# Another order of the first steps, and other due times, in a fused linear-attention and feed-forward kernel

## The chip, the cores and the metric

The kernel runs on one core of one Trainium2 chip. The metric is the time of one execution on the device in microseconds. The times of the kernel before are 523.04, 523.28 and 522.9 us, median 523.04. Profiles are of one execution; their times count from the first instruction.

## The reference

A gated linear attention over 4 batches, 8 heads, 768 steps and heads of 48, then a feed-forward layer with a squared ReLU over the 3072 tokens of 384 numbers that the attention leaves.

```python
for t in range(S):                                   # attention: q, k, v, alpha are (4, 8, 768, 48)
    state = alpha[:, :, t, :, None] * state + einsum('bhd,bhe->bhde', k[:, :, t], v[:, :, t])
    y[:, :, t] = einsum('bhd,bhde->bhe', q[:, :, t], state)
x = y.transpose(0, 2, 1, 3).reshape(3072, 384)
h = maximum(x @ w_in, 0.0)                           # w_in (384, 2048)
out = (h * h) @ w_out                                # w_out (2048, 384), both given in float64
```

## The kernel before

**Blocks.** The attention is cut into 24 blocks of 128 steps: block n is chunk n // 4 of batch n % 4. In a block the decays are handled by logarithms. `ln` takes them (ACT, line 242), `cs` sums them over the steps with a triangular matrix on TensorE, `eb` and `ei` make the factors b and 1/b from the sums on ACT, `mq` and `mk` multiply q and k by them on VectorE (line 284). `qT` and `kT` turn q and k on TensorE, `qc` and `kc` copy them out of PSUM. `sc` makes the scores, `kv` the sums of the state, `am` copies the scores through a mask, `us` adds the state, and `st` (next_state, line 414) makes the state of the next chunk. For `st` the last row of b is needed as a column: `bl` writes that row to DRAM (line 297, "row"), `br` reads it back spread over partitions (line 303, "last"), in two DMAs of single numbers. `ya` and `yb` make the output of two blocks, `ev` copies it out of PSUM into x, the operand of the feed-forward layer (line 515), by ACT and, for the first two pairs, also by VectorE. b lies in two buffers that take turns (line 275), so `eb` of block n waits until `mq` and the row of block n - 2 are done with one.

**Groups.** Four blocks, one of each batch, make a group: 512 tokens. The feed-forward layer takes group after group, six in all, 16 columns j of w_in of 128 each, then the product with w_out. While TensorE works on group g, the attention of group g + 1 is made between its matmuls.

**Weights.** The float64 weights come in 16 pieces of 768 KB and are turned into float32 by `first` and `second` on VectorE (lines 153 to 182) with `middle` on ACT between them (lines 166, 169). Group 0 uses them as float32 matmuls of two passes each (line 805, line 701 with w_out), but for a last part. From group 1 on, the numbers are split into a large and a small part and their difference (`prepare`, line 580: cast_w and scale_w on ACT, rest_w and diff_w on VectorE), and a product is three float32r passes (line 622, line 701). The split weights are kept in DRAM and streamed back by SP (`stream`, `pump`). x and h are split too (`split_x`, `split_h`, `diff_h`, on ACT and VectorE).

**What sets the order.** The kernel writes out its own schedule; every engine works its instructions off in the order in which the program gives them, SP its DMA issues too.

- The first four blocks are a list of words (line 851). A word is a step and its block: `mk0` is mk of block 0, `load2a` loads alpha of block 2, `weights0` loads the next piece of weights, `first0`, `middle0`, `second0` turn piece 0, `ha1` and `hb1` are the first and second half of the 512 tokens for column 1, `zeros2` is a filler: a matmul by zeros, three times, six passes in the trace (line 338); `warm0` is one more (line 221).
- From then on `weave` (line 923) goes through a list of units of TensorE's work, each with a cost, and puts steps with a due time between them. Units in groups 1 to 5 are some 1.3 us. `attention` (line 889) gives the due times of a pair of blocks from a start t: the turn of q and k (`turn`, line 474) at 6.5, their eight copies (line 490) at 7, `ga` (scores and sums of the first block, and the output of the pair before) and `gb` (the same of the second) at the values in AT, or at 9.5 and 10.5 times a scale in group 0.
- AT (line 19) holds the numbers. `g0`, `g1`, `g`: starts of the pairs in group 0, group 1 and later ones. `sc0`: scale in group 0. `w_first`, `w_in_at`, `w_in_by`, `wstep`, `o0`, `o2`: when the pieces of weights are split. `g0x`, `g1x`, `xs`: when x of the next group is split. `h0`, `h1by`, `s0`, `ahead`: how early h is split. `str1`: when a stream begins. `tp`: for each of four columns, in groups 2 to 5, which engine squares: with A, ACT scales in PSUM, takes the ReLU and squares; with M, VectorE squares; with D, ACT copies out and VectorE adds, takes the ReLU and squares. `evs0`: spacing of the evictions in group 0. `late` is used only if group 0 is float32 throughout, which it isn't.

Of the kernel before, what the change touches and what calls it, by code (L numbers as in the profile page):

```python
# [15 lines left out]


GB = 4
AT = {'evs': 0.4, 'lead': 4, 'post': 3, 'w_first': (46.0, 49.5, 53.0), 'wstep': 1.6, 'w_in_at': 2, 'w_in_by': 3.4, 'room1': 22, 'room': 25, 's0': 4, 'ahead': 6, 'late': 2, 'xs': 0.2, 'g0': (-0.5, 19.5, 28.0), 'sc0': (2.35, 2.35, 2.35), 'g1': (2.5, 19.5, 35.0), 'g': (2.2, 15.0), 'g1x': 50, 'gx': 46, 'g0x': 55.5, 'k0': 2, 'h0': 18, 'k1': 4, 'h1': 4, 'h1by': 2, 'evs0': 0.8, 'tp': 'ADMD', 'tp1': 'ADAD', 'split': 8, 'o0': (40, 47), 'o1': (), 'o2': (23, 26, 29, 35, 42, 36), 'str1': 24, 'ga': 10, 'gb': 12.5}


RUN = {0: 128, 32: 32, 64: 64, 96: 32}
# [3 lines left out]
def kernel(  # L26
# [220 lines left out]

    SPLIT = AT["split"]

# [290 lines left out]
    here, todo, room = {}, [], [22]  # L540
# [27 lines left out]
    def diff_w(w, p):  # L568
# [5 lines left out]
        for x in "ld":  # L574
            t = made.pop((x, w, p))
            if w == "i" or p >= NW - AT["k0"] or (x == "l" and p >= NW - AT["k1"]):
                here[x, w, p] = t
        pump()

    def prepare(at, w, p):  # L580
        step = AT["wstep"]
        fs = (cast_w, rest_w, scale_w, diff_w)
        return [(at + i * step, f, (w, p)) for i, f in enumerate(fs)]
# [78 lines left out]
    def splits_of_x(at, g):  # L662
        return [(at + i * AT["xs"], f, (g, i % KM)) for i, f in enumerate((split_x,) * KM + (diff_x,) * KM)]

    def layer_in(g):
        units = []
        for n in range(NJ + 2):
            if n < NJ:
                units.append((1.05, in_x, (n,)))
            if 0 <= n - 2 < NJ:  # L670
                units.append((0.53, in_y, (n - 2,)))
            if 0 <= n - AT["post"] < NJ:
                units.append((0, in_post, (n - AT["post"],)))
            if AT["lead"] <= n < AT["lead"] + AHEAD and (g > 1 or AT["k1"] == NW):
# [145 lines left out]
    def ffn_out(g, t, i):  # L820
# [28 lines left out]
    steps["hb"] = lambda j: ffn_in(0, j, slice(HT, 2 * HT))  # L849
    steps["first"], steps["middle"], steps["second"] = convert_first, convert_middle, convert_second  # L850
    first = """
        ln0 cs0 ei0 mk0 warm0 eb0 bl0 mq0 kT0 load0v kc0 ln1 qT0 load2a load2k cs1
        eb1 qc0 mq1 sc0 bl1 kv0 qT1 load1v ei1 mk1 load2q load3a kT1 ln2 qc1 load3k
        cs2 br0 am0 kc1 eb2 sc1 weights0 br1 us0 kv1 zeros2 bl2 load2v am1 ei2 us1
        load3q ya0 ln3 cs3 yb0 eb3 weights1 mk2 ei3 load3v mq2 qT2 st0 ev0 kT2
        zeros2 zeros2 zeros2 kc2 first0 mk3 middle0 kT3 mq3 br2 load4v qc2 kc3 bl3
        weights2 qT3 sc2 load4q qc3 kv2 second0 am2 br3 first1 sc3 weights3 us2
        load4a kv3 am3 us3 load4k middle1 ha1 second1 ya2 yb2 ev2 weights4 first2
        ha0 hb1 middle2 hb0 st2 st3 st1
    """  # L860
    for word in first.split():
        f = max((x for x in steps if word.startswith(x)), key=len)
# [167 lines left out]
```

## Time and profile before

| what | us |
|---|---|
| median of three runs | 523.04 |
| span of the profiled execution | 520.6 |
| difference, outside the span | 2.4 |
| TensorE busy | 510.8 |
| VectorE busy | 366.0 |
| ACT busy | 313.0 |
| end of the last matmul | 517.1 |

The page's first part gives the busy time of each engine, the second its share in 40 slices of 13 us. The list of who waited for whom has four parts: the instruction that waited, what released it, and then the sum, the number of times and the longest. A line of a timeline has start, duration, engine, line of the kernel, operation and tiles; behind "x" the number of instructions that were put together, and in brackets the idle time before them and what ended it. The chain of waits has start, duration and name. In a stage table each engine has its busy time in the stage; the last numbers are the granted clock, the share of the 16 DMA engines and GB/s.

### The profile page before, as it was taken

What the parts mean: (1) busy time and instruction counts of PE and PEld (TensorE: products, weight loads), DVE (VectorE), ACT (ScalarE), POOL (GpSimd) and SP (SyncE); (2) the same over time, 40 slices, a digit from 0 to 9 for tenths busy, and PEclk for the clock granted to TensorE, in tenths of its full rate; (3) what the DMA queues carried; (4) which work ended last, traced back from release to release, by engine and by line L of the source; (5) the groups of instructions that cost most, each with busy time, mean ns of one, the idle gap of its engine ahead of it and who ended that gap; (6) DMA issues with size and microseconds to landing.
All of it is one profiled execution on the core that took longest, in us unless ns stands there. A gap on an engine that the chain in (4) does not pass through costs nothing.

```text
span 520.6 us, 12925 instructions
## 1 busy us (share of the span) xinstructions
PE 510.8 (98%) x5276; PEld 418.2 (80%) x5276; DVE 366.0 (70%) x631; ACT 313.0 (60%) x650; POOL 5.4 (1%) x29
## 2 busy tenths in 40 slices
PE   7989999999999999999999999999999999999997
PEld 4754455668887668988899988899988899988997
DVE  4798989979978787867597476587465476363861
ACT  4668785677888594575963275963275763164620
POOL 4000000000000000000000000000000000000000
PEclk9999999999999999999999999999999999999999
DMA  9999687244686787898884788964673534898201
GB/s 161 209 278 213 196 240 218 60 114 176 224 200 196 195 246 198 264 317 206 195 248 148 251 246 198 230 187 150 231 255 126 179 126 151 268 340 293 70 0 62
DMA packets 140995, 102.36 MB, mean 197 GB/s; under 512 B 111476, under 2 KB 114568, under 8 KB 140936
## 3 DMA queue, kind: packets, MB, share of 16 engines
q1 hardware_dynamic: 140936, 101.53, 68.3%
q8 instruction: 42, 0.69, 0.6%
q14 instruction: 17, 0.14, 0.1%
HBM read 84.18 MB, written 17.33 MB: 195 GB/s over the span
## 4 chain that ended last, share of the span: by engine, by line
PE 93%; DVE 2%; SPq 2%; DMA 1%; issue 1%; POOL 1%; ACT 0%; POOLq 0%; DVEq 0%
PE o L701 41%; PE h L622 32%; PE h L805 7%; PE y L352 4%; PE T L482 2%; PE sckv L372 2%; PE sckv L395 2%; PE cs L265 1%; DMA qk_lent<-in_q_dram 1%; SPq L303 1%; SPq L109 1%; PE cs L268 1%; PE cs L269 1%; DVE x L515 0%; DVE w_in L182 0%
## 5 line engine op out<-in xcount | busy, mean ns | idle before, releaser
L622 PE MATMUL h<-xa,wb 128*128 128x512 f32 x240 | 68.2, 392 | 0.0
L622 PE MATMUL h<-xl,wl 128*128 128x512 f32 x240 | 67.9, 391 | 0.0
L622 PE MATMUL h<-xd,wd 128*128 128x512 f32 x240 | 67.3, 396 | 0.0
L515 ACT COPY x<-y 32x256 f32<-32x256 f32 (+2 forms) x132 | 47.2, 366 | 25.4 <-PE y L352 20.1
L547 DVE TENSOR_TENSOR hid<-h,hid 128x512 f32<-128x512 f32 x40 | 27.6, 689 | 45.5 <-PE h L622 45.4
L701 PE MATMUL o<-wb,ha 128*128 128x384 f32 x160 | 54.6, 342 | 0.0
L701 PE MATMUL o<-w_out,hid 128*128 128x384 f32 x160 | 54.0, 491 | 0.0
L701 PE MATMUL o<-wd,hd 128*128 128x384 f32 x304 | 53.8, 334 | 0.0
L701 PE MATMUL o<-wl,hl 128*128 128x384 f32 x160 | 53.5, 335 | 0.0
L639 ACT ACTIVATE h<-h 128x512 f32<-128x512 f32 x40 | 23.3, 582 | 49.7 <-PE h L622 49.7
L622 PEld LDWEIGHTS h<-xl,wl 128*128 128x128 f32 x240 | 45.1, 188 | 10.0 <-DVE xl L547 0.4
L701 PEld LDWEIGHTS o<-wd,hd 128*128 128x128 f32 x304 | 52.7, 188 | 0.3 <-DVE osb L737 0.3
L622 PEld LDWEIGHTS h<-xa,wb 128*128 128x128 f32 x240 | 44.6, 188 | 9.3 <-ACT xa L596 0.2
L622 PEld LDWEIGHTS h<-xd,wd 128*128 128x128 f32 x240 | 44.2, 188 | 9.2
L701 PE MATMUL o<-wb,hx 128*128 128x384 f32 x144 | 48.7, 338 | 0.0
L701 PE MATMUL o<-wl,hx 128*128 128x384 f32 x144 | 48.1, 334 | 0.0
L701 PEld LDWEIGHTS o<-w_out,hid 128*128 128x128 f32 x160 | 29.8, 190 | 19.3
L637 ACT ACTIVATE hid<-h 128x512 f32<-128x512 f32 x40 | 24.0, 600 | 34.6 <-PE h L622 34.5
L805 PE MATMUL h<-x,w_in 128*128 128x512 f32 (+1 forms) x108 | 43.6, 552 | 1.2 <-ACT x L515 1.2
L596 ACT ACTIVATE ha<-hid 128x512 fp32r<-128x512 f32 x40 | 25.6, 639 | 25.5 <-DVE hx L547 16.1
L805 PEld LDWEIGHTS h<-x,w_in 128*128 128x128 f32 x108 | 19.9, 190 | 21.1 <-issue 17.2
L547 DVE TENSOR_TENSOR hl<-hid,ha 128x512 fp32r<-128x512 f32 x40 | 27.5, 688 | 10.1 <-ACT ha L596 10.1
(114 smaller groups left out, 879.7 us busy)
## 6 DMA issues: line engine op xcount, KB each, us to landing
wd<-do SPq DMA_DIRECT2D x36, 384.0 KB, 3.7
wl<-lo SPq DMA_DIRECT2D x34, 384.0 KB, 4.0
wl<-li SPq DMA_DIRECT2D x32, 384.0 KB, 3.5
wd<-di SPq DMA_DIRECT2D x32, 384.0 KB, 3.9
raw<-in_moe_w_in_dram SPq DMA_DIRECT2D x8, 768.0 KB, 5.6
raw<-in_moe_w_out_dram SPq DMA_DIRECT2D x8, 768.0 KB, 5.6
v_in<-in_v_dram SPq DMA_DIRECT2D x24, 192.0 KB, 4.7
out_dram<-osb SPq DMA_DIRECT2D x24, 192.0 KB, 1.9
```

Of the source, the lines that this page charges most:

```text
L352: ins = nc.tensor.matmul(out=ys[e][64 * half : 64 * half + D + G * e, m % 2, p // 2, t], lhsT=lhsT, rhs=rhs, start=(half, e) not in seen, ...
L372: nc.tensor.matmul(out=ps[e][HALF[h], 0, p, :], lhsT=ks[rows, p, HALF[h]], rhs=qs[rows, p, HALF[h]], start=True, stop=True, skip_group_che ...
L395: nc.tensor.matmul(out=ps[h][64 * e : 64 * (e + 1), 1, p, G:64], lhsT=tile_of("k", n)[HALF[h], 2 * p + e, :], rhs=tiles["v"][n % NV][HALF[ ...
L482: nc.tensor.transpose(out=ps[h][:, i, p, :], in_=rows[HALF[h], 128 * p : 128 * (p + 1)], identity=ident[HALF[h], HALF[h]],)
L515: copy(out=x[kk][to : to + m, t : t + 2], in_=blk[n]["y"][e][r : r + m, :, p // 2],)
L547: nc.vector.tensor_tensor(out=o, in0=x, in1=z, op=op)
L596: nc.scalar.activation(out=a, in_=x, func=AF.Copy, scale=NEAR)
L622: nc.tensor.matmul(out=acc["h", j], lhsT=here[w, "i", p][:, kk, jj * 128 : (jj + 1) * 128], rhs=x_parts[x][:, kk], start=start and kk == 0 ...
L637: nc.scalar.activation(out=hid[j], in_=x, func=AF.Copy, scale=E)
L639: nc.scalar.activation(out=x, in_=x, func=AF.Copy, scale=1.0 + E)
L701: nc.tensor.matmul(out=acc[t][:, 0:DM], lhsT=lhs[:, t * C : (t + 1) * C], rhs=rhs, start=start, stop=stop, skip_group_check=True,)
L805: nc.tensor.matmul(out=ps, lhsT=w[:, kk, c0 : c0 + 128], rhs=xT[g][kk][:, cols], start=(kk == 0), stop=(kk == KM - 1),)
```

## The change

The list of the first steps is put in another order, with five fillers of zeros for four and without `warm0`, and numbers in AT are changed. No step of the computation is added or taken away, but with `tp` DDMD for ADMD the columns 0, 4, 8 and 12 of groups 2 to 5 go from A to D.

In the new list row 1 (`bl1`) is issued behind the first weights, `cs3` and `cs2` stand ahead of `ya0`, `ev2` stands ahead of `second1`, `ha1` and `ha0` behind `yb2`, and the loads of block 3 ahead of the second piece of weights.

```diff
-AT: w_first (46.0, 49.5, 53.0), wstep 1.6, w_in_at 2, w_in_by 3.4, s0 4, ahead 6, late 2, xs 0.2,
-    g0 (-0.5, 19.5, 28.0), sc0 (2.35, 2.35, 2.35), g1 (2.5, 19.5, 35.0), g1x 50, g0x 55.5, h0 18,
-    h1by 2, evs0 0.8, tp 'ADMD', o0 (40, 47), o2 (23, 26, 29, 35, 42, 36), str1 24, ga 10, gb 12.5
+AT: w_first (46.67, 46.11, 53.52), wstep 1.47, w_in_at 2.47, w_in_by 3.41, s0 2, ahead 20, late 1, xs 0.0,
+    g0 (-0.15, 20.48, 28.0), sc0 (2.35, 2.26, 2.35), g1 (5.52, 23.0, 35.06), g1x 51.48, g0x 56.25, h0 15,
+    h1by 1, evs0 1.07, tp 'DDMD', o0 (40.37, 47.68), o2 (29.94, 22.86, 12.71, 31.3, 38.86, 26.77),
+    str1 15.34, ga 8.47, gb 12.26
     first = """
-        ln0 cs0 ei0 mk0 warm0 eb0 bl0 mq0 kT0 load0v kc0 ln1 qT0 load2a load2k cs1
-        eb1 qc0 mq1 sc0 bl1 kv0 qT1 load1v ei1 mk1 load2q load3a kT1 ln2 qc1 load3k
-        cs2 br0 am0 kc1 eb2 sc1 weights0 br1 us0 kv1 zeros2 bl2 load2v am1 ei2 us1
-        load3q ya0 ln3 cs3 yb0 eb3 weights1 mk2 ei3 load3v mq2 qT2 st0 ev0 kT2
-        zeros2 zeros2 zeros2 kc2 first0 mk3 middle0 kT3 mq3 br2 load4v qc2 kc3 bl3
-        weights2 qT3 sc2 load4q qc3 kv2 second0 am2 br3 first1 sc3 weights3 us2
-        load4a kv3 am3 us3 load4k middle1 ha1 second1 ya2 yb2 ev2 weights4 first2
-        ha0 hb1 middle2 hb0 st2 st3 st1
+        ln0 load0v zeros2 cs0 ei0 eb0 zeros2 mk0 kT0 mq0 bl0 load3a load2a load1v ln1
+        br0 cs1 eb1 ei1 qT0 load2k load2q weights0 zeros2 mq1 qc0 kc0 bl1 qT1 sc0 kv0
+        qc1 mk1 kT1 kc1 sc1 am0 load3k us0 st0 load3q ln3 kv1 am1 ln2 us1 cs3 cs2 eb3
+        load2v ya0 ei2 yb0 mk2 eb2 ei3 mq2 zeros2 load3v weights1 kT2 ev0 first0 load4a
+        qT2 mk3 middle0 kT3 mq3 qT3 kc2 bl3 zeros2 qc2 second0 br1 sc2 qc3 kc3 bl2 sc3
+        br2 am2 kv3 am3 kv2 us2 us3 ya2 yb2 first1 st1 middle1 ev2 second1 ha1 br3 ha0
+        st2 weights2 weights3 load4v hb1 load4q first2 st3 load4k hb0 middle2 weights4
     """
```

(The numbers of AT that stay are left out.)

More of the change, by code (lines that the diff above doesn't have):

```diff
@@ L18 @@
 GB = 4
-AT = {'evs': 0.4, 'lead': 4, 'post': 3, 'w_first': (46.0, 49.5, 53.0), 'wstep': 1.6, 'w_in_at': 2, 'w_in_by': 3.4, 'room1': 22, 'room': 25, 's0': 4, 'ahead': 6, 'late': 2, 'xs': 0.2, 'g0': (-0.5, 19.5, 28.0), 'sc0': (2.35, 2.35, 2.35), 'g1': (2.5, 19.5, 35.0), 'g': (2.2, 15.0), 'g1x': 50, 'gx': 46, 'g0x': 55.5, 'k0': 2, 'h0': 18, 'k1': 4, 'h1': 4, 'h1by': 2, 'evs0': 0.8, 'tp': 'ADMD', 'tp1': 'ADAD', 'split': 8, 'o0': (40, 47), 'o1': (), 'o2': (23, 26, 29, 35, 42, 36), 'str1': 24, 'ga': 10, 'gb': 12.5}
+AT = {'evs': 0.4, 'lead': 4, 'post': 3, 'w_first': (46.67, 46.11, 53.52), 'wstep': 1.47, 'w_in_at': 2.47, 'w_in_by': 3.41, 'room1': 22, 'room': 25, 's0': 2, 'ahead': 20, 'late': 1, 'xs': 0.0, 'g0': (-0.15, 20.48, 28.0), 'sc0': (2.35, 2.26, 2.35), 'g1': (5.52, 23.0, 35.06), 'g': (2.2, 15.0), 'g1x': 51.48, 'gx': 46, 'g0x': 56.25, 'k0': 2, 'h0': 15, 'k1': 4, 'h1': 4, 'h1by': 1, 'evs0': 1.07, 'tp': 'DDMD', 'tp1': 'ADAD', 'split': 8, 'o0': (40.37, 47.68), 'o1': (), 'o2': (29.94, 22.86, 12.71, 31.3, 38.86, 26.77), 'str1': 15.34, 'ga': 8.47, 'gb': 12.26}
 RUN = {0: 128, 32: 32, 64: 64, 96: 32}
```

## The prediction

> **What bounds the kernel now.** I read the page first (busy shares, slices), then who waited for whom on TensorE, the chain of waits up to 45 us, and the timelines of the engines over the same stretch.
>
> ```profile
> span 520.6 us, 12925 instructions
> ...
> PE 510.8 (98%) x5276; PEld 418.2 (80%) x5276; DVE 366.0 (70%) x631; ACT 313.0 (60%) x650; POOL 5.4 (1%) x29
> ...
> PE   7989999999999999999999999999999999999997
> ```
>
> TensorE is busy 98% of the span, and 90% or more of every slice between the third and the last. Its instructions stay the same but for fillers, so time can only come out of its waits, or out of new ones. Its waits:
>
> ```profile
> PE h L805 <- ACT x L515: 1.2, 3, 0.7
> PE warm L221 <- POOL s L67: 1.1, 1, 1.1
> PE y L352 <- issue: 1.0, 1, 1.0
> ```
>
> The span less the busy time is 9.8 us. Of it 3.5 us are the stores after the last matmul (517.1), 1.0 us is the wait named "issue" at 203 us, which no semaphore explains, 5.0 us lie before 35.3 us, and 0.3 are scattered. In that first stretch fillers hide more. The chain of waits there, start and duration of each piece:
>
> ```profile
> 18.25 5.06 DMA qk_lent<-in_q_dram
> ...
> 23.81 0.95 DVE power L175
> 24.76 0.88 DVE w_in L179
> 25.66 0.96 DVE w_in L182
> ...
> 31.18 0.96 DVE w_in L182
> ...
> 32.17 0.42 DVE x L515
> ...
> 35.29 9.72 PE h L805 x26
> ```
>
> A load is followed by VectorE alone. VectorE's timeline has it working without a break of 0.3 us from the eviction of blocks 0 and 1 (18.87, six copies) to 41.5:
>
> ```profile
> 17.86 0.36 DVE L421 TENSOR_TENSOR s<-s,last 128x192 f32<-128x192 f32 x1 [1.41 <-DMA last<-row]
> 18.87 2.65 DVE L515 COPY x<-y 32x256 f32<-32x256 f32 x6 [0.65 <-PE y L352]
> ```
>
> From 35.29 TensorE runs through. 26 passes stand there: 8 halves of 0.216 us are left of columns 0 and 1, so **column 2 (j=2) starts at 35.29 + 1.7 = 37.0 us**. This time, less what waits come after it, is what the change can move.
>
> **Part 1, the order of the first four blocks.** I call X the start of VectorE's eviction ev0 (18.87 now) and ask when X comes and how long column 2 is behind it.
>
> *X.* In the new order three things lie ahead of it. (a) Two fillers stand around cs0, six passes each. While the first passes run, one takes 2.93/6 = 0.49 us, later 1.56/6 = 0.26:
>
> ```profile
> 1.09 2.93 PE L221 MATMUL warm<-s 128*128 128x256 f32 x6 [1.09 <-POOL s L67]
> 4.33 1.62 PE L265 MATMUL cs<-a_in,causal 128*128 128x384 f32 x2 [0.31 <-POOL causal_r L204]
> ...
> 14.11 1.56 PE L338 MATMUL zeros<-s 128*128 128x256 f32 x6
> ```
>
> So the first filler ends at about 3.8 + 5 x 0.43 + 0.26 = 6.2, cs0 then takes 0.81 (the later rows' time) and ei0 starts at 7.05 rather than 5.99; b of block 0 is there at 7.9. (b) In SP's queue row 0 waits for that b, and behind it now stand a3, a2, v1, last 0 (two), k2, q2, the first weights, and only then row 1; before, row 1 was issued at 9.45, ahead of all of these but a2 and k2. (c) ACT's eb2 writes the buffer of b that row 1 is read from, so it waits until row 1 has landed; mq2 needs eb2, and ev0 stands behind mq2 on VectorE. A small load moves 197 KB; between 2 and 7 us the DMA engines moved 199 GB/s, between 11 and 15 us 187: 1.03 us each. The weights move 786 KB at 344 to 377 GB/s (18:20, 24:25): 2.2 us. v0 landed at 10.3. Then 5 loads (5.2), the weights (2.2), last (0.3, by its 384 small pieces against a load's 1024), and 0.4 of gap while SP waits for b: row 1 lands at 18.4. eb2 0.45, mq2 0.5: **X = 19.35**, 0.5 later than now. ln3 and ln2, which now wait for a3 until 16.70, no longer set it.
>
> [...]
>
> *Behind X.* VectorE's queue, with the rows' spacing: ev0 2.65, first half of weights 0 1.0, mk3 and mq3 1.0, second half 2.75, both masks (am2, am3) 1.35, us2 and us3 0.75 with the wait for kv2: 9.5. The products end 1.73 behind us3, as now (29.42 to 31.15): X + 11.2. ev2 follows at once (2.65), because the second half of weights 1 now stands behind it (2.8): X + 16.7. TensorE meanwhile does columns 0 and 1 in one run (24 halves, 5.2 us, X + 16.4), where it now has 1.2 us of waits for x. So column 2 starts at X + 16.7 = 36.05, against 37.0 now (X + 18.1): **-0.95 us**. Its next need, weights 2, comes at X + 22.0 on VectorE against X + 21.8 on TensorE, within 0.2, and weights 3 at X + 26.1 against 27.0: nothing is given back. The two extra filler matmuls (6 passes more of zeros, 2 fewer of warm) lie ahead of loads and are in X.
>
> *Bounds.* If SP stalls as it does now at last 0 (2.31 us for one issue, DMA then at 84 GB/s in 15:18), row 1 lands 1.5 later: +0.55. If row 1 isn't what ends last, X is 18.15 (us1 behind last 0, y behind it): -2.1.
>
> **Part 2, the splits of x ahead of group 1.** Now xa starts at 126.28, and TensorE loses 0.26 us at 128.1 to 128.9. Between the end of the products and xa, ACT has 12 evictions of 0.365 and two weight steps of 0.73; in the new order one of the two stands behind xa, and the distance on TensorE stays 6.9 us: **-0.3** (bounds -0.3 and 0).
>
> **Part 3, attention nearer to its turn.** ga moves from 10 to 8.47 units behind the start of its pair. Counted in the order of instructions, between turn and scores there are now 18 passes of 0.227 us in groups 2 to 4, and 9 after the change; in group 1's first turn 9 become 12. ACT's eight copies must end first:
>
> ```profile
> 255.75 0.72 ACT L490 COPY qs<-T 128x256 f32<-128x256 f32 x2
> ```
>
> The turn starts at 253.41, the copies end at 256.47, 3.06 behind it; the scores come at 253.41 + 1.15 + 9 x 0.227 + 0.1 = 3.3 behind it (5.50 now). That still fits by 0.2. In group 1 the copies of the turn at 141.00 begin at 143.55, some 1.8 us late, because ACT is loaded (33.99 us of 40 in 120:160). There the two moved pieces of w_out add four steps of each engine, but the pair is 3 units later and has 12 passes: by ACT's sum in the new order the copies are 0.1 to 0.2 late. **+0.15** (bounds 0 and +1.6).
>
> **Part 4, the rest.** DDMD puts 16 tiles on VectorE: 1.2 us less of ACT, 1.37 more of VectorE each. In 220:260 VectorE has 26.05 us of 40, so 5.5 more are hidden. Earlier splits (ahead 20, s0 2): in the last group VectorE's first hx part is done at 485.8 and used at 487.8; the new order puts 0.69 ahead of a later part, still 1.3 early. Other moved weights, streams and the times of group 0: nothing, as VectorE and ACT had idle time around them; if that cover is gone it shows in the bound of part 3.
>
> **The sum.** -0.95 - 0.3 + 0.15 = -1.1. The profiled execution has a span of 520.6, the median of the runs is 523.04; the 2.4 us outside the span stay. 519.5 + 2.4: **521.9 us**, own range 521.0 to 522.8.
>
> **The rivals.** 0.2% is 1.05 us, about what a measurement of this kernel can tell from no change: the lines are 522.0 and 524.1.
>
> 1. *The queue runs dry.* SP stalls at last 0 as now; X 20.85; 0.55 - 0.15 = +0.4: 523.4. For it: the 84 GB/s. Against: only three loads, not four, are ahead of last 0. 0.14.
> 2. *Row 1 is early or the idle at 203 goes.* X 18.15, -2.1 - 0.15: 520.8; with the 1.0 us as well 519.8. 0.20.
> 3. *Slower: the copies miss the scores.* ga has lost 2 us of distance in each of eight turns. It decides from the point where ACT reaches its copies over 0.2 us later than at 253.41. If it is 0.5 late in each: 8 x 0.5 = +4.0: 525.9; in group 1 alone +1.6: 523.5. For it: 1.8 us late at 141.00. Against: ACT loses 19 us of work in the later groups. 0.18.
> 4. *The slow passes last longer.* Then the new first filler ends at 6.4, cs0 takes 1.64 as now and not 0.81, and SP's queue behind b is 1.0 later: 522.9. Against: the passes after 5.75 are fast now, although TensorE then had a gap of 0.31. 0.06.
>
> [...]
>
> **Chances.** Forecast 0.42 (0.27 of it below 522.0), rivals 0.14, 0.20, 0.18, 0.06. Faster: 0.27 + 0.20 = 0.47; slower: 0.18 and 0.04 of rival 1, 0.22; the same 0.31. The range leaves out 0.07 below 519.9 and some 0.11 above 525.0.
>
> **What would show it.** The start of column 2 at 36 us; eb2 at 18.4, released by a DMA (row 1); ev0 at 19.4; no wait for xa; scores 3.3 us behind each turn without a wait for ACT. It is wrong if column 2 comes after 37, if eb2 isn't what mq2 waits for, or if TensorE shows waits for L490.

## The result, and the profile after

The changed kernel takes 526.4 us (median of 17 runs, 524.59 to 528.3), the kernel before beside it 523.15 (17 runs, 522.71 to 524.79): ratio 1.0064, 95% interval 1.0054 to 1.0073. It is slower by 3.3 us where 1.1 less was forecast. The runs of the changed kernel spread over 3.7 us, those of before mostly over 1. The profiled execution took 528.3 us and is the slowest of them, so its times stand for the bad end; the changed kernel was run again later, with a second profile (e19 below). Four of the twelve runs of one experiment below (e10) fell in a slower state of the chip, at 531.96 to 536.46 us, and its figures go by the other eight.

The page of the changed kernel: span, busy time, and the busy tenths in 40 slices of 13 us.

```profile
span 526.2 us, 12942 instructions
...
PE 512.0 (97%) x5280; PEld 421.1 (80%) x5280; DVE 383.6 (73%) x663; ACT 296.2 (56%) x618; POOL 5.3 (1%) x29
...
PE   8699999999999998999999999999999999999997
```

TensorE's busy time rose by 1.2 us, its idle time from 9.8 to 14.2. The second slice fell to 6. Who waited for whom on TensorE:

```profile
PE kT L309 <- DVE qk_lent L284: 3.5, 1, 3.5
PE y L352 <- issue: 2.7, 3, 1.4
PE warm L221 <- POOL s L67: 1.1, 1, 1.1
PE qT L309 <- DVE qk_lent L284: 0.7, 1, 0.7
PE sckv L372 <- ACT ks L325: 0.7, 1, 0.7
```

Two entries are new in size: one wait of 3.5 us of the transposes of block 3 for VectorE, and three waits named "issue" where there was one of 1.0. Starts of the stages in the two profiles, worked out from TensorE's instructions:

| start of | before | after | difference |
|---|---|---|---|
| column 2 | 37.12 | 40.53 | +3.41 |
| group 1, x times w_in | 127.60 | 130.84 | +3.24 |
| group 1, h times w_out | 166.34 | 168.73 | +2.39 |
| group 2, x times w_in | 217.29 | 221.75 | +4.46 |
| group 3, x times w_in | 296.57 | 302.03 | +5.46 |
| last matmul's end | 517.08 | 522.62 | +5.54 |

So the head (up to column 2) loses 3.4, group 1's first half gains 0.9, its second half loses 2.1, group 2 loses 1.0, and from there nothing changes. The two halves of group 1 together lose 1.2, as much as the waits named "issue" grew in them (2.15 against 0.96).

**The head.** SP's queue, then ACT's and VectorE's timelines of the changed kernel:

```profile
12.89 2.55 SPq L126 DMA_DIRECT2D raw<-in_moe_w_in_dram  x1
15.53 0.29 SPq L297 DMA_DIRECT2D row<-b  x1
```

```profile
19.85 0.49 ACT L276 ACTIVATE b<-cs 128x384 f32<-128x384 f32 x1 [2.82 <-DMA row<-b]
```

```profile
20.37 0.56 DVE L284 TENSOR_TENSOR qk_lent<-qk_lent,b 128x384 f32<-128x384 f32 x1 [2.75 <-ACT b L276]
20.96 2.65 DVE L515 COPY x<-y 32x256 f32<-32x256 f32 x6
```

The chain is the predicted one: row 1 behind the first weights, eb2 released by row 1, mq2 by eb2, ev0 behind mq2. But the issue of the weights alone held SP for 2.55 us, row 1 landed at 19.76 instead of 18.4, and X (the start of ev0) is 20.96 instead of 19.35. TensorE's timeline behind it:

```profile
21.07 0.63 PE L309 MATMUL qT<-ident,qk_lent 128*128 128x128 f32 x4 [0.73 <-DVE qk_lent L284]
25.19 0.94 PE L309 MATMUL kT<-ident,qk_lent 128*128 128x128 f32 x4 [3.49 <-DVE qk_lent L284]
25.93 1.06 PE L309 MATMUL qT<-ident,qk_lent 128*128 128x128 f32 x4
26.78 2.48 PE L338 MATMUL zeros<-s 128*128 128x256 f32 x6
...
33.44 1.37 PE L352 MATMUL y<-am,v_in 64*48 64x64 f32 x52 [0.50 <-issue]
```

Six filler passes take 2.48 us here; before they took 1.56. The stage table shows why:

```profile
20.00:25.00 5.00, 0.97 (x8) 0.52 (x5) 4.45 (x10) 3.67 (x9) 0.00 (x0) 1.00 1.04 161
25.00:30.00 5.00, 4.81 (x67) 4.07 (x70) 3.36 (x6) 3.07 (x6) 0.00 (x0) 0.66 0.58 148
```

TensorE is busy for 0.97 us of five, and in the next five its granted clock is 0.66. In the old order 18 filler passes stood in just this wait; TensorE's timeline before:

```profile
19.67 4.05 PE L338 MATMUL zeros<-s 128*128 128x256 f32 x18
23.56 0.60 PE L309 MATMUL kT<-ident,qk_lent 128*128 128x128 f32 x4
```

The trace records the fall itself: the clock stood at 0.5 from 25.42 to 28.83, 3.41 us. Work that takes 3.41 us at half speed takes 1.7 at full speed: by this estimate one such fall costs up to 1.7 us.

**The waits named "issue".** TensorE's timeline at the largest, at the end of group 1:

```profile
205.05 0.66 PE L352 MATMUL y<-am,v_in 64*48 64x64 f32 x28
207.15 0.33 PE L352 MATMUL y<-am,v_in 64*48 64x64 f32 x3 [1.44 <-issue]
```

It stands in the middle of equal instructions; no semaphore is involved. The page lists a queue that brings instructions:

```profile
q8 instruction: 42, 0.69, 0.6%
```

42 packets of 16 KB. I counted TensorE's records in the trace (matmuls, weight loads and 156 waits for semaphores and drains, in order of their starts, from 0; 10,716 in all, 255 to a packet). In this profile the waits stand at records 962, 3777 and 4545, and that of the kernel before at 4546. Divided by 256 these all leave 193 or 194. **So the waits stand where one block of 256 instructions ends and the next has not come**; the packet ahead of the wait at 205.7 began at 204.94, and the wait ended at 207.15. The packets can be counted too: in all 20 profiles of this document the first one in the profile goes with record 449 (193 + 256), the second with 705, and so on. Each of them began when 17 to 299 of the records ahead of its block were still to start, never earlier, and no block began less than 2.20 us behind the start of its packet. By these two numbers a stretch that works off its last 299 records in less than 2.20 us has to wait.

### The profile page after: what moved, and what is told of

Its sections match the earlier page's. It is cut to its first block, busy times and chain, and to the rows that moved or that the text cites. A ratio compares the mean times of both kernels' runs of the same rounds, so it can differ in the third digit from the quotient of the medians.

```text
span 526.2 us, 12942 instructions
## 1 busy us (share of the span) xinstructions
PE 512.0 (97%) x5280; PEld 421.1 (80%) x5280; DVE 383.6 (73%) x663; ACT 296.2 (56%) x618; POOL 5.3 (1%) x29
## 4 chain that ended last, share of the span: by engine, by line
PE 88%; DVE 3%; SPq 2%; DMA 2%; ACT 2%; issue 1%; POOL 0%; DVEq 0%; POOLq 0%; ACTq 0%
PE o L701 40%; PE h L622 28%; PE h L805 7%; PE y L352 4%; PE T L482 2%; PE sckv L372 2%; PE sckv L395 2%; DMA last<-row 1%; SPq L303 1%; DVE x L515 1%; DMA row<-b 1%; PE zeros L338 1%; SPq L109 1%; PE cs L265 1%; PE warm L221 1%
## 5 line engine op out<-in xcount | busy, mean ns | idle before, releaser
L637 ACT ACTIVATE hid<-h 128x512 f32<-128x512 f32 x56 | 33.5, 599 | 81.9 <-PE h L622 81.7
L547 DVE TENSOR_TENSOR hid<-h,hid 128x512 f32<-128x512 f32 x56 | 38.5, 687 | 38.3 <-PE h L622 38.2
L701 PE MATMUL o<-wl,hx 128*128 128x384 f32 x144 | 48.1, 334 | 0.0
L651 DVE SCALAR_TENSOR_TENSOR hid<-hid 128x512 f32<-128x512 f32 x56 | 37.3, 683 | 0.1
L547 DVE TENSOR_TENSOR osb<-o,osb 128x384 f32<-128x384 f32 x24 | 12.9, 554 | 25.3 <-PE o L701 24.1
```

Of the source, the lines that this page charges most:

```text
L547: nc.vector.tensor_tensor(out=o, in0=x, in1=z, op=op)
L637: nc.scalar.activation(out=hid[j], in_=x, func=AF.Copy, scale=E)
L651: nc.vector.scalar_tensor_tensor(out=h, in0=h, scalar=0.0, in1=h, op0=ALU.max, op1=ALU.mult)
L701: nc.tensor.matmul(out=acc[t][:, 0:DM], lhsT=lhs[:, t * C : (t + 1) * C], rhs=rhs, start=start, stop=stop, skip_group_check=True,)
```

## The experiments

The theory after the two traces: the loss is made of (1) the late X, (2) half speed behind TensorE's empty wait, (3) blocks of instructions that end in dense stretches. The rivals: another part of the new list costs it (B), or the numbers by their own work (C). All results in one table; the times of before beside them are 522.9 to 523.3. "Issue" is the sum of those waits after 100 us in the profile, the clock that of 25 to 30 us.

| run | median, us | lowest to highest | ratio, 95% | column 2 | clock | issue |
|---|---|---|---|---|---|---|
| before | 523.15 | 522.71 to 524.79 | | 37.12 | 1.00 | 1.0 |
| the change | 526.40 | 524.59 to 528.30 | 1.0054 to 1.0073 | 40.53 | 0.66 | 2.2 |
| e1 row 1 early | 526.48 | 524.65 to 527.12 | 1.0045 to 1.0075 | 38.71 | 0.76 | 2.8 |
| e2 list only | 523.52 | 521.71 to 524.58 | 0.9996 to 1.0017 | 37.08 | 1.00 | 0 |
| e3 numbers only | 524.21 | 523.14 to 525.66 | 1.0021 to 1.0039 | 37.55 | 1.00 | 1.6 |
| e4 fillers | 521.82 | 520.90 to 523.19 | 0.9970 to 0.9987 | 36.46 | 1.00 | 0.6 |
| e5 stream shifted | 525.99 | 525.01 to 529.00 | 1.0044 to 1.0089 | 43.58 | 0.63 | 0.5 |
| e6 row 1 early, fillers | 521.62 | 521.24 to 523.45 | 0.9962 to 0.9985 | 36.64 | 1.00 | 1.1 |
| e7 fillers, old numbers | 522.31 | 522.04 to 523.17 | 0.9980 to 0.9998 | 38.24 | 1.00 | 0 |
| e8 before, shifted | 522.75 | 522.33 to 523.46 | 0.9988 to 1.0005 | 39.33 | 1.00 | 0 |
| e9 fillers moved | 525.68 | 524.07 to 527.20 | 1.0027 to 1.0062 | 40.04 | 1.00 | 2.5 |
| e10 moved, row 1 early | 525.22 | 523.51 to 531.14 | 1.0023 to 1.0075 | 36.66 | 1.00 | 3.6 |
| e11 before, no fillers | 524.11 | 522.49 to 525.59 | 1.0009 to 1.0034 | 38.80 | 0.51 | 0.5 |
| e12 no first filler | 523.53 | 522.41 to 524.88 | 0.9995 to 1.0017 | 37.17 | 1.00 | 2.0 |
| e13 as e10, shifted | 522.22 | 521.23 to 528.81 | 0.9972 to 1.0019 | 36.33 | 1.00 | 0.7 |
| e14 as e6, shifted | 521.50 | 520.76 to 522.46 | 0.9963 to 0.9983 | 37.08 | 1.00 | 0.5 |
| e15 attention far | 524.01 | 521.45 to 525.34 | 0.9998 to 1.0025 | 40.17 | 0.66 | 1.0 |
| e17 before, halves | 521.40 | 521.14 to 522.46 | 0.9959 to 0.9983 | 38.00 | 1.00 | 0 |
| e18 all mended | 520.73 | 520.35 to 521.50 | 0.9949 to 0.9973 | 37.13 | 1.00 | 0 |
| e19 the change again | 527.44 | 524.72 to 530.59 | 1.0057 to 1.0113 | 39.84 | 0.74 | 3.7 |

### e1: row 1 ahead of the weights

```diff
-br0 cs1 eb1 ei1 qT0 load2k load2q weights0 zeros2 mq1 qc0 kc0 bl1 qT1 sc0 kv0
+br0 cs1 eb1 bl1 ei1 qT0 load2k load2q weights0 zeros2 mq1 qc0 kc0 qT1 sc0 kv0
```

> The changed kernel, with the load of row 1 (step bl1) put ahead of the first weights' loads on SP's queue. Theory T1 (the loss at column 2 comes from row 1, issued behind the weights, and from TensorE's half speed after its long wait): row 1 lands before 17.5, eb2 and VectorE's ev0 start 2 us earlier or more, column 2 starts at 35.5 to 37.5 instead of 40.5, and the time is 521.5 to 523.5. Rival B (the rest of the list's new order costs it, such as ev2 ahead of second1): column 2 stays at 39 or later and the time at 525 or above. Rival C (the numbers at which attention, weights and streams are placed cost it): column 2 gets earlier, but groups 1 and 2 still add about 2 us, and the time is 524.5 to 525.5.

X came at 19.41 and column 2 at 38.71, yet the time is that of the change, 526.48. That row 1 set X in the change is confirmed: eb2 now waits for no DMA, and X is set by the output y. Its price is not: TensorE still waited 1.93 us ahead of kT3, and still came out of it slow (clock 0.76, filler passes 2.56 us for six), and later there were three issue waits, 2.8 us together. The late X alone is not the loss.

### e2 and e3: the list alone, the numbers alone

Each is the changed kernel with one half of the change undone: e2 has the old AT, e3 the old list.

> Only the new order of the steps; the numbers of attention, weights and streams as before. T1: column 2 at 40 to 40.5, group 1 starts 3.2 later than before, and the time is 525.5 to 527. Rival C: column 2 is late, but it is made up behind, and the time is about 523. The wait for xa ahead of group 1 (0.25 us) should be back.

> Only the new numbers of attention, weights and streams; the steps in the old order. T1: column 2 at 37.1, the time 523 to 524.5 (the prediction's own sum for the numbers alone is -0.15). Rival C: 525 to 526, with the instruction-fetch waits of 0.5 to 1.5 us in TensorE's row and 0.57 us ahead of group 2's output.

The list alone costs 0.6 (523.52, with an interval that holds no change too), the numbers alone 1.3 (524.21), both together 3.3 to 4.5: they do not add up. In e2's profile the wait ahead of kT3 was 2.00 us and the clock stayed full; that run took 522.25, while the runs of e2 with a mean clock of 0.997 took 523.3 to 524.6. In e3 column 2 is at 37.55, as with the old list, and the loss comes later: two issue waits, 1.6 together, at records 3777 and 6081, so again at 193 of 256.

### e4: fillers in the empty wait

```diff
-qT2 mk3 middle0 kT3 mq3 qT3 kc2 bl3 zeros2 qc2 second0
+qT2 zeros2 zeros2 mk3 middle0 kT3 mq3 qT3 kc2 bl3 zeros2 qc2 second0
```

> The changed kernel with two filler steps on TensorE more, behind qT2, where TensorE stood idle for 3.5 us ahead of kT3; row 1 as late as in the changed kernel. T1's second part (half speed after the idle time): the granted clock stays at 1.000, the transposes follow each other at 0.11 us and the filler ahead of the scores takes 1.5 us instead of 2.5, column 2 starts at about 39, and the time is about 1.4 us below the changed kernel's, with less spread between runs. Rival: the half speed is not on the path, column 2 stays at 40.5 and the time at 526.

521.82: 4.6 less than the change, by two steps that compute nothing, and 1.1 less than before. With the same list otherwise, rival B has no price left. TensorE's timeline and the stage:

```profile
20.40 2.76 PE L338 MATMUL zeros<-s 128*128 128x256 f32 x12
23.41 0.63 PE L309 MATMUL kT<-ident,qk_lent 128*128 128x128 f32 x4 [0.26 <-DVE qk_lent L284]
23.88 0.60 PE L309 MATMUL qT<-ident,qk_lent 128*128 128x128 f32 x4
24.32 1.46 PE L338 MATMUL zeros<-s 128*128 128x256 f32 x6
```

```profile
25.00:30.00 5.00, 4.24 (x196) 3.62 (x194) 4.71 (x12) 1.96 (x4) 0.00 (x0) 1.00 0.32 39
```

The same six passes take 1.46 us. From ev0 (19.09) to column 2 (36.46) it is 17.4 us, against 19.6 in the profile of the change. This gives some 2.2 of the 4.6, with the wait of 0.50 named issue at 33.44 in it. X itself came 1.9 earlier than in that profile, by the run (below). The rest cannot be the clock in the head: the fillers also push all later instructions 24 records on in TensorE's stream, and the issue waits fell from 2.2 to 0.6.

### e5 and e8: the stream shifted, head disturbed

The first three filler matmuls of the program are cut so that there are 12 passes more; in e5 in the changed kernel, in e8 in the kernel before.

```diff
-    for _ in range(3):
-        warm(0)
+    for parts in (1, 4, 4):
+        warm(0, parts)
```

> The changed kernel, whose first three filler matmuls are cut: two of the three become four narrow ones each, the same columns in all. Nothing else differs, but every later instruction of TensorE stands 24 records (12 passes with their weight loads) further on in its stream, as in the run with fillers. Theory I (part of the loss are waits at fixed places of TensorE's instruction stream, every 256 records, where the next block of instructions has not come): the waits named issue at 181.8 (0.9) and 205.5 (1.4) shrink to under 0.8 together, TensorE's long wait ahead of kT3 and its half speed stay, and the time is 524.2 to 525.4. Rival (only the half speed counts, the waits named issue are something else): 526.4 as in the changed kernel.

> The kernel before, with the same cut of its first three filler matmuls, so that TensorE's stream is shifted by 24 records. Theory I: the wait named issue at 203 (1.0) shrinks to 0.5 or less, and the time falls by 0.4 to 0.9, to 522.0 to 522.5. Rival: unchanged, 522.9.

Both miss, for a reason of their own: a pass of 64 columns takes 0.21 us in the slow stretch at the start, half of one of 256 (0.43) and not a quarter, so the cut added time, and the slow passes lasted longer. cs0 began at 8.09 instead of 5.67 in e5, at 5.42 instead of 4.33 in e8. What can be read lies behind column 2: in e8 the stretch from there to the end of the last matmul is 478.8 us, in the kernel before 480.0, and the wait of 1.0 at 203 is gone. In e5 it is 478.7 against 482.1 of the change, and the issue waits fell to 0.5. Theory (3) holds there, but these two runs alone would not carry it.

### e6 and e7: both mends; fillers with the old numbers

e6 is e4 with the edit of e1, e7 is e4 with the old AT.

> The fillers behind qT2, and row 1's load ahead of the first weights. If row 1's landing still sets the start of ev0 once the clock is kept: ev0 0.5 to 0.9 earlier than with the fillers alone, column 2 at 35.4 to 36.0, and the time at 520.6 to 521.4. Rival (what stands ahead of row 1, the sums cs1 and eb1, sets it in most runs): the time of the fillers alone, 521.8.

> The new order with the fillers behind qT2, with the old numbers of attention, weights and streams. Rival C (the new numbers cost time by their own work): the time falls below that of the fillers with the new numbers by 1 to 2.9, to 519 to 520.8. Theory I (the numbers cost by where the instruction blocks' ends fall, not by their work): the time within 0.7 of 521.8, and the difference is read off as waits named issue in groups 1 and 2.

e6: X at 18.29, 0.8 earlier than in e4, yet column 2 only at 36.64, in part because of an issue wait of 0.6 in the head; 521.62, the time of the fillers alone. That is the rival's time, though not its mechanism, since X did come earlier: with the clock kept, row 1's place is not worth a measurable amount. e7: 522.31, within 0.7 of e4. Rival C falls: the numbers do not cost by their work, since with the stream shifted the new numbers are no slower than the old.

### e9, e10 and e12: fillers moved instead of added

```diff
-ln0 load0v zeros2 cs0 ei0 eb0 zeros2 mk0 kT0 mq0 bl0
+ln0 load0v cs0 ei0 eb0 mk0 kT0 mq0 bl0
 ...
-qT2 mk3 middle0 kT3 mq3 qT3
+qT2 zeros2 zeros2 mk3 middle0 kT3 mq3 qT3
```

That is e9; e10 has row 1 early too; e12 is e4 with only the filler ahead of cs0 left out.

> The changed kernel with its first two filler steps (around cs0 and mk0) moved behind qT2. The number of TensorE's records ahead of group 1 is that of the changed kernel, so its instruction blocks end at the same places of the work. Two causes (half speed, and the blocks' ends): the clock stays at 1.000, cs0 starts at 4.3 to 4.8, column 2 at 35.5 to 37, but the waits named issue near 182 and 205 stay at 0.8 and 1.2 or more: 521.8 to 523.6, above the time of the fillers that were added (521.8), though the start is earlier. If the blocks' ends do not matter: no such waits, 520.5 to 521.5. If the early fillers are needed for the clock's rise: passes of 0.427 up to 7 and later, and no gain over 526.

> As the run before, with row 1's load ahead of the first weights. Row 1 is then in no run behind a weights issue that stalls (2.3 to 2.6 us in two of five profiles with row 1 behind it, 0.7 to 1.0 in the others): the median 0.2 to 0.9 lower than without it and the spread smaller. Rival: ev0 is set by y and the products ahead of it, no difference.

> The kernel with the fillers behind qT2, without the filler step ahead of cs0 (six passes that stand between the first loads and cs0 at half speed). cs0 starts at 4.3 to 4.8 instead of 5.5 to 6.4; if the sums of block 0 set row 1 and so ev0, column 2 comes 0.5 to 1.5 earlier, and the time is 520.3 to 521.5; the blocks' ends move by 12 records, up to 1 either way. Rival: the loads set the start (v and the next alphas), and nothing changes: 521.8.

e10 is the telling one. Its head is as good as e6's (column 2 at 36.66 and 36.64, clock 1.00), and it still takes 525.22, 3.6 more than e6. The two differ in two filler steps at the start, 24 records. Its waits named issue are 3.6 us, at records 3777, 4545 and 6081. The last of them, and the stage table behind it:

```profile
258.75 0.64 PE L352 MATMUL y<-qs,us 48*48 48x64 f32 x29
261.25 0.21 PE L352 MATMUL y<-qs,us 48*64 48x64 f32 x1 [1.87 <-issue]
```

```profile
260.00:265.00 5.00, 3.75 (x42) 3.04 (x42) 2.21 (x4) 0.58 (x2) 0.00 (x0) 0.75 0.81 214
265.00:270.00 5.00, 5.00 (x114) 4.61 (x112) 4.05 (x8) 3.40 (x8) 0.00 (x0) 0.91 0.44 145
```

**Behind the issue wait of 1.87 us the clock fell too** (0.75, then 0.91): the two causes feed each other. From group 2's start to its product with w_out it is 48.1 us here, 44.1 before and 44.3 in e13, which has the same work and no such wait: the wait of 1.87 cost 3.8, itself and the 3.41 us of half speed behind it (262.49 to 265.90). Against its expectation e10 is 0.5 below e9, within the noise, and its spread is not smaller. e9 has the same waits (2.5) and 525.68, where 521.8 to 523.6 was expected; it also met one in the head, at record 449, so that y, X (21.70) and column 2 (40.04) came late. e12 is shifted by 12 records only, has waits of 2.0 at the records 3778 and 4546, and takes 523.53. Its column 2 (37.17) is no earlier than e4's, so the filler ahead of cs0 is not what sets the head; the expectation missed.

### e11: the kernel before without its fillers

```diff
-zeros2 zeros2 zeros2 kc2 first0 mk3 middle0 kT3 mq3 br2 load4v
+kc2 first0 mk3 middle0 kT3 mq3 br2 load4v
```

> The kernel before without its three filler steps ahead of kc2 (18 passes, at 19.7 to 23.7). If a wait of TensorE that is left empty costs by the clock alone: the passes behind it start at half speed, transposes at 0.21 instead of 0.11, a granted clock under 0.95 in 25:30, column 2 at 37.8 to 39.5 instead of 37.1, the time 523.5 to 525.5 (the instruction blocks' ends move by 36 records too, worth up to 1 either way). Rival: the fillers cover nothing, and column 2 comes at 37.1 or earlier, since they no longer delay kT3.

```profile
23.38 1.09 PE L309 MATMUL kT<-ident,qk_lent 128*128 128x128 f32 x4 [3.36 <-DVE qk_lent L284]
24.38 1.12 PE L309 MATMUL qT<-ident,qk_lent 128*128 128x128 f32 x4
25.43 1.13 PE L372 MATMUL sckv<-qs,ks 48*64 48x64 f32 x32
```

```profile
25.00:30.00 5.00, 5.00 (x134) 4.46 (x133) 4.59 (x11) 2.18 (x4) 0.00 (x0) 0.51 1.08 255
```

The old order, with the wait left empty, shows the same: 3.36 us idle, clock 0.51, column 2 1.7 later, 524.11. The fillers are part of the schedule's speed although they compute nothing.

### e13, e14, e17: the stream shifted, and nothing else

Behind qT2 (in e17: ahead of kc2) each filler matmul is cut into two halves: 128 columns instead of 256, the same time in all, 12 passes more (e17: 18). e13 is e10 with this edit, e14 is e6, e17 is the kernel before.

```diff
-    for _ in range(3): nc.tensor.matmul(out=ps[:, 0:NP, :], ..., rhs=s_t[3], ...)
+    for i in range(6):
+        some = slice(i % 2 * NP // 2, (i % 2 + 1) * NP // 2)
+        nc.tensor.matmul(out=ps[:, some, :], ..., rhs=s_t[3][:, some, :], ...)
```

> The run with the moved fillers and the early row 1, its six filler matmuls behind qT2 cut into halves: the same columns and, going by the narrow ones' 0.11 us at full speed, the same time, but 12 passes more, so that all later instructions stand 24 records further on. If the places where the instruction blocks end cost the time: no waits at 178 and 259, that at 201 under 1.0, the time 520.8 to 522.3 where 526.3 was, and the spread gone. Rival (the fillers around cs0 and mk0 make the difference in another way, such as the phase of the clock): 524 to 527 again.

> The run with both edits (521.6), its fillers behind qT2 cut into halves in the same way: 48 records further on than in the changed kernel. If the blocks' ends cost: the remaining wait at 200 (1.2) shrinks again or goes, 520.3 to 521.6, unless an end falls into another dense stretch (a wait of 0.5 to 1.5 at a new place, at a record that leaves the same rest by 256). Rival: 521.6 unchanged.

> The kernel before with its nine filler matmuls ahead of kc2 cut into halves: the same columns, 18 passes and 36 records more, in a wait that is there anyway. If the blocks' ends cost: the wait named issue at 203 (1.0) shrinks or goes, nothing else changes, column 2 at 37.1, and the time is 522.0 to 522.5 where 523.0 was. Rival: 523.0 unchanged.

e13 takes 522.22 where e10 took 525.22: 24 records, 3.0 us. (One of its 11 runs is at 528.81, so its interval is wide, but it stays clear of e10's.) The stretch in which e10 waited 1.87:

```profile
256.51 0.61 PE L362 MATMUL y<-qs,us 48*48 48x64 f32 x29
256.92 0.22 PE L362 MATMUL y<-am,v_in 64*48 64x64 f32 x1
256.94 0.24 PE L362 MATMUL y<-qs,us 48*64 48x64 f32 x2
256.96 0.68 PE L362 MATMUL y<-am,v_in 64*48 64x64 f32 x31
```

No wait. e14 takes 521.50 (48 records); its gain over e6 is too small to be told. And e17: the kernel before, with nothing but nine matmuls cut in two, goes from 523.0 to 521.40, ratio 0.9959 to 0.9983. TensorE's timeline at the same 30 matmuls, first before, then in e17:

```profile
202.45 0.64 PE L352 MATMUL y<-am,v_in 64*48 64x64 f32 x27
204.05 0.33 PE L352 MATMUL y<-am,v_in 64*48 64x64 f32 x3 [0.96 <-issue]
```

```profile
203.31 0.68 PE L362 MATMUL y<-am,v_in 64*48 64x64 f32 x30
```

The wait is gone, and e17's profile has no other of its kind. That profile is of the slowest of e17's six runs (522.46), in which the clock fell at 7.33 behind a wait of 1.44 us, so that column 2 came at 38.00 and not at the 37.1 expected; from there to the last matmul it is 479.1 us against 480.0. The gain of the median, 1.6, is more than the one wait of 1.0, and more than expected; where the rest comes from is not shown.

### e15, e18, e19: the attention's distance; all mended; the change again

e15 is the change with ga 10 and gb 12.5 as before; e18 is e14 with these two; e19 is the change, unchanged.

> The changed kernel with attention's distance to its turn as before (10 and 12.5 units, for 8.47 and 12.26); all else as in the change. If the nearer attention makes the stream denser and so the waits named issue: those near 182 and 262 go, that near 205 stays near the 1.0 of before, and the time falls by 1 to 2 from 526.4, to 524.4 to 525.4 (the head's loss stays). Rival (the other numbers, such as the later start of group 1's pairs, do it): the waits stay, 526 to 527.

> The run with fillers in halves and the early row 1 (521.5), with attention's distance as before (10, 12.5). If the three causes are all of the loss: no wait named issue of over 0.7, column 2 at 36.3 to 37.1, and the time at 520.0 to 521.3, below the kernel before by 1.7 to 3. If the ends of the blocks meet a new dense stretch: 521.5 to 523, with a wait at a record of the same rest by 256.

> The changed kernel once more, unchanged. If the first profile's late row 1 (issued 2.55 behind the first weights) is a matter of the run: in this one row 1 may be issued at 13.4 to 14 instead of 15.5, ev0 start at 19.0 to 20, column 2 come at 38.5 to 39.5 with the half speed of 25:30 still there. If it belongs to the order: ev0 again at 20.5 or later, column 2 at 40 or later. The time 526.4 in both cases.

e15: 524.01, 2.4 less than the change, although the head is as bad in its profile (column 2 at 40.17, clock 0.66). Of the issue waits one of 1.0 is left, as in the kernel before. Why the nearer attention matters can be read from how long 255 records of a block last (from the trace): those up to record 6081 take 2.4 us in the change, 2.2 in e10 and 4.3 in e15, those up to 3777 take 1.9, 1.9 and 2.3; in e13 both take over 4. In all profiles the issue waits after 100 us stand behind blocks that lasted 1.8 to 2.9 us. But not every such block has one (e17 has two of 1.85 us without), so here a fast block is needed, not enough: it also counts how early its packet began (with 129 records still to start in e10's wait at 4545, with 287 in e17 at that block, which had none).

e18: 520.73, ratio 0.9949 to 0.9973, the fastest kernel here, with a spread of 1.2. TensorE's waits in its profile:

```profile
PE warm L221 <- POOL s L67: 1.1, 1, 1.1
PE sckv L382 <- ACT ks L325: 0.7, 1, 0.7
PE y L362 <- DVE us L416: 0.6, 1, 0.6
PE h L815 <- DVE w_in L182: 0.4, 1, 0.4
PE sckv L382 <- DVE ks L325: 0.3, 1, 0.3
```

Both new entries of the change are gone. e19 gives the second profile of the change (528.55 us): the weights' issue took only 0.82 and row 1 was issued at 14.52, but the slow passes at the start lasted longer, so that row 0 was issued at 8.50 instead of 7.42, and X is 20.51 all the same. The wait ahead of kT3 is 2.9, the clock 0.74, and there are three issue waits, 3.7 us together, after 100 us. What varies from run to run is which of these events comes and how hard.

## Why the prediction was wrong

*What bounds the kernel.* Right: only TensorE's waits moved the time. But the wait named issue at 203 was noted as one "which no semaphore explains" and only counted as something that could go. It was a place in the instruction stream (record 4546), and an edit ahead of it that adds records moves the place (by 36 records in e17, where the wait is gone). This view was there before the change.

*X.* Mechanism right, size off: 19.35 forecast, 20.96 and 20.51 in the two profiles. The term that failed is "row 1 lands at 18.4" (19.76 in the first): in the first profile the issue of the weights held SP for 2.55 us, where I had counted only transfers; in the second the slow start, which I had made rival 4, delayed row 0. In e4, the same order up to there, X was 19.09. I had allowed for an early row 1 (rival 2). In the traces, with row 1 behind the weights in the queue, its completion came ahead of the last of the weights' sixteen in seven of nine profiles, by up to 1.1 us (17.89 and 18.98 in e4), and 0.07 behind it in the first profile of the change (19.76 and 19.69). Row 1 was late there by its issue.

*Behind X.* Here the prediction failed first. "X + 9.5" for the products holds where the clock is kept: in e4 they start 28.62 - 19.09 = 9.5 behind X. In the change it is 11.1. The old order had 18 filler passes in the wait of TensorE ahead of kT3; the new order has fillers at the start in their place, which I counted as "in X", and I asked nothing of the wait that was left empty. It was 3.5 us, the clock fell, and the passes behind it ran at half speed. e11 shows the same in the old order, e4 the way back. Column 2 was forecast at X + 16.7; it is X + 19.6 in the change and X + 17.4 in e4. Most of that last difference is the products' length: they end 2.1 us behind their start in e4, where 1.73 was taken from the kernel before, in which half of the first of them ran ahead of us3.

The clock fell behind waits of 3.49 (the change), 3.5 (e5 and e15), 3.36 (e11) and 2.9 (e19), and also behind 1.93 (e1), 1.87 (e10) and 1.44 (e17), and did not behind 2.00 (e2), 1.51 (e19) and 1.44 (the change, at 207). So in these runs a wait below 2 us is not safe, and its length alone does not tell. It stayed at half for 3.41 us in six profiles and for 6.83 in two (e5, e11).

*Part 2.* Right: from the first pass of group 1 to the seventh it is 1.39 us, where it was 1.64; the wait for xa, 0.25, is gone.

*Part 3.* Its mechanism was right (the copies end 3.06 behind the turn, the scores come 3.45 behind it, and no wait for line 490 is seen; 3.06 and 3.3 were forecast; in the first turn of group 1 the copies end later, at 4.09, and no wait is seen either), its price wrong: +0.15 with a bound of +1.6, where e15 gives 2.4. The distance took nine wide passes out from between two runs of small matmuls, so that a block of instructions was worked off faster than the next came. Rival 3 had nearly the time (525.9) by a mechanism that did not occur.

*The sum.* With the clock kept, the stream shifted, row 1 early and the distance as before, the change takes 520.73; the kernel before with its stream shifted 521.40, in another series of runs with nearly the same time of before (523.02 and 522.92). The work of the new order and numbers by itself may then be worth some -0.6, on the side of the forecast; the two intervals overlap, so this is not shown. The loss is in two things that the sum had no term for, and the mean clock that is noted for each run tells their shares roughly. Four of the 17 runs of the change had 0.999 or more and took 524.59 to 525.43; the 13 others had 0.995 to 0.997 (one fall of 3.41 us in 526 makes 0.997) and took 525.72 to 528.30. Between the medians lie 2.0 us. So the change with its clock kept still loses 1.6 of the 3.3, and the issue waits are what the profiles show for it. The runs of e15 part in the same way, into 522.24 and 524.38. In e4, e6, e7, e14 and e18, which have fillers in the wait, none of 46 runs is below 0.999. The shares aren't independent, since an issue wait can bring the clock down too (e10).

*Left open.* Why some packets begin with 129 records to go and others with 287; what decides whether the clock falls behind a wait of 1.4 to 2 us, and whether runs of small matmuls count as idle time for it (the waits of 1.93, 1.87 and 1.44 us stand near such runs or transposes; not tried); and the wait of 0.41 us ahead of the product at 267 in the first profile of the change, which its second does not have.

## What to carry to other kernels

Before fillers are moved, find the wait that they stand in and ask how long TensorE would be empty there: in these runs the clock fell behind waits of 1.44 to 3.5 us, which by the estimate above cost up to 1.7 us more, and twice that in two profiles (e5, e11). A wait that no semaphore explains, in the middle of equal small matmuls, is worth a count of the instructions ahead of it: if several leave the same rest by 256 (here 193 or 194), cutting fillers in two moves them all, and took 1.6 us from a kernel whose work was left alone (e17). When two halves of a change do not add up, and the runs spread more than those of before, look for such waits first.

## What was not expected of the hardware

- TensorE's instructions came in packets of 16 KB (42 for 10,716 records in the change, 0.69 MB). In the 17 profiles that have a wait named issue of over 0.3 us, every one of these stands at a record with the rest 193 or 194 by 256; the longest is 1.9 us (e10). Each packet took 0.9 to 2.2 us, and such a wait ended 2.2 to 3.0 us behind the start of one (204.94 to 207.15 in the change, 258.31 to 261.25 in e10).
- A filler pass of 64 columns took half the time of one of 256, not a quarter (0.21 and 0.43 us in the slow stretch at the start, e5); halves of 128 columns cost 0.08 us more in all (24 in 2.84 us in e14, 12 of 256 in 2.76 in e4).
- The issue of the first load of weights on SP took 2.55, 2.33 and 2.10 us in three profiles of the new order (the change, e5, e15), 1.79 and 1.81 in two (e6, e13), and 0.68 to 1.06 in ten others.
- The clock fell to half for 3.41 us (the change, e1, e10, e15, e17, e19) or 6.83 (e5, e11), however long the wait ahead of it had been (1.44 us in e17, 3.5 in e5 and e15).
